# Block-sparse attention and a gated convolution FFN on one core: the two middle batches convolved whole, in a token order shared by q and k

## The chip, the cores and the metric

The kernel runs on one core of a Trainium2 chip. The time is the device time of one execution in microseconds (us). Six runs of the kernel before gave 215.57 us as median (214.54 to 216.39). One execution was profiled: 216.15 us, of which the span from the first to the last instruction is 214.4 us. The granted TensorE clock was 0.999.

## The reference

Inputs: q, k and v of shape (4, 8, 768, 64) in float32, a table of three sampled key blocks for each of 24 query blocks, and three FFN weights. Cut to what matters:

```python
scores = (q @ k.T) / sqrt(64)                       # per batch and head, 768 x 768
mask = |qblock - kblock| <= 1 or block in {0, 23} or sampled
attn = softmax(where(mask, scores, -1e9))
x = (attn @ v) heads side by side                   # (4, 768, 512)
h = relu(x @ w_in)                                  # (4, 768, 1024)
conv[s] = cw[0]*h[s-1] + cw[1]*h[s] + cw[2]*h[s+1]  # along the tokens, per channel
out = (h * sigmoid(conv)) @ w_out                   # (4, 768, 512)
```

The kernel computes all 768 x 768 scores. It adds the mask in the score matmul itself: rows 64 to 87 of the operands hold, for each token, an indicator of its block on the key side and the mask values of its block on the query side. The sigmoid is computed as a tanh of half the argument.

## The kernel before, in words

**Halves and units.** The work is cut into 8 halves (`n`): batch `b` and token half `g`. A half is 18 *units* of eight 128x128 score blocks: score matmuls into a PSUM tile `st` (L678), one exponential over 128x1024 on ACT (L685) into `pt`, and eight matmuls of the probabilities with v into `av` (L705). Units are numbered from 0 to 143 through the kernel. After 4.5 units a pair of heads is complete: DVE takes the reciprocal of the row sums (L629) and scales the result into `xtok` (L631), which SP turns by a transposing DMA into `xT` (L652); for the first half, PE turns it.

**Heads.** For each of 16 pairs of heads (`P`), POOL issues the q, k and v loads, which also cast to bf16 (L492). The q and k of the first `NPE` = 6 pairs are transposed by PE and copied by DVE (L533, L539). For later pairs SP issues two transposing DMAs into a staging tile `tmp` (L581), and DVE copies it into the slot's tiles `et` and `ot` (L424). There are `NSLOT` = 6 slots. The mask rows of slots 2 to 5 are copied from slot 0 by SP's DMAs (L445).

**Token order.** k and v put tokens 6p to 6p+5 on partition p. q puts tokens 3p to 3p+2 of each half there, so that the tokens of one half lie in three columns of 128.

**FFN of a half.** 8 blocks of 128 channels. FFN1 is four matmuls of 384 tokens (L729), then a relu on ACT or DVE (L740, L742) into `hE`. For a pair of blocks POOL adds the neighbours at the edges of the three columns (L829 to L835), and DVE forms the convolution: per tap two 384-wide multiplies (L753), two 768-wide adds (L759); ACT takes a tanh (L769); DVE adds 1 (L772) and multiplies by `hE` into `gT` (L781). The last token of half 0 needs the first of half 1, so it is saved (L844) and joined later by four small instructions (L859 to L867). FFN2 is eight matmuls for each of three token blocks (L799), a copy to `o2s` and a store by SP (L340).

**What sets the order.** All of this is put down as operations with a duration, a priority, dependencies and buffers (`Op`, `Buf`, `Pool_`). `Scheduler.forward` plays it through with one queue per engine, and one called `DQ` for the DMA engines; `backward` gives new priorities from the ends that follow; this is repeated `PASSES` = 12 times. The engines' programs are then written in the planned order, and each engine carries out its program in that order. So constants such as `OFF` (when a half's FFN is due), `XLAT` and `TLAT` (what a transposing DMA is thought to take after its issue), `load_u` (the unit at which a pair's loads may be issued) or the buffer counts change the order of instructions on all engines, and their waits.

Of the kernel before, what the change touches and what calls it, by code (L numbers as in the profile page):

```python
# [24 lines left out]
class Op:  # L25
    __slots__ = ("alts", "fn", "deps", "prio", "lat", "allocs", "earliest", "pend", "outs", "ready",
                 "start", "end", "eng", "key", "uses")

    def __init__(self, alts, fn, prio, deps, lat, earliest):
        self.alts, self.fn, self.prio = alts, fn, prio  # L30
        self.deps = deps
        self.lat = lat
        self.allocs, self.uses = [], []
        self.earliest = earliest
        self.outs = []
        self.start = self.end = self.eng = None
# [12 lines left out]
FLEX = 0.0345  # L49
LAT = {"PE": 0.23, "ACT": 0.20, "DVE": 0.16, "POOL": 0.20, "SP": 0.0, "DQ": 1.9}  # L50
OWN = {"PE": 0.0, "ACT": 0.12, "DVE": 0.11, "POOL": 0.10, "SP": 0.0, "DQ": 0.0}


class Scheduler:
# [22 lines left out]
    def forward(self):  # L77
# [11 lines left out]
        while left:  # L89
# [27 lines left out]
            for e, t in free.items():  # L117
                be = None
                for o in cand:
# [5 lines left out]
                    k = (s, o.prio, o.key)  # L125
                    if be is None or k < be[0]:
                        be = (k, o, e)
                if be is not None:
                    k2 = (be[0][0], be[0][1], be[0][2], be[0][0] + be[1].alts[e])
                    if best is None or (k2[0], k2[3]) < (best[0][0], best[0][3]):  # L130
                        best = (k2, be[1], e)
            if best is None:
                raise RuntimeError("no order: buffers too few")
            k, o, e = best
            o.eng = e
            o.start = k[0]
            o.end = k[0] + o.alts[e]
# [25 lines left out]
    def backward(self, order):  # L163
# [25 lines left out]
        while ready:  # L189
# [4 lines left out]
            for j in pred[i]:  # L194
                pend[j] -= 1
                if not pend[j]:
                    ready[j] = max(0.0, max(end[m] + lat for m, lat in succ[j]))
        for o, t in zip(order, end):
            o.prio = -t
            o.outs = []  # L200
            for b in o.allocs:
# [12 lines left out]
def kernel(  # L214
# [22 lines left out]
    NPE = 6  # L237
    NWARM = 34

# [19 lines left out]
    NTMP, NVN, NNAT, NPT, NXK, NXT, NHE, NCV, NGT, NOS = 2, 3, 3, 5, 3, 4, 3, 3, 4, 4  # L259
# [7 lines left out]
    hE_t = many(NHE, [128, NFFC, 640], BF16, "hE")  # L267
    m_t = many(NCV, [128, 2, 768], BF16, "m")
    tn_t = many(NCV, [128, 768], BF16, "tn")
    gT_t = many(NGT, [128, NFFC, 384], BF16, "gT")  # L270
# [11 lines left out]
    bblkn = sb.tile([NB, 6, 128], BF16, tag="bblkn", name="bblkn")  # L282
# [36 lines left out]
    T0, PACE0, PACE1 = 8.0, 0.91, 1  # L319
    OFF = 32.0894  # L320
    XLAT, TLAT = 3.908, 9.2201
    S_FIRST, A_FIRST, R_FIRST, N_FIRST = 5.6663, -4, 0.1178, 0.842
    F1S, F2A, F2S = 0.03, 2.344, 0.191
    WO = 22.9467
    OFFL = 28
# [12 lines left out]

    def dma_h(dst, src):
        return lambda e: (nc.sync if e == "SP" else nc.scalar).dma_start(out=dst, in_=src() if callable(src) else src)  # L340

    def src_of(t, b, h):

        if t is q:
# [7 lines left out]
    def dst_of(t, tile_, pair):  # L352
        if t is not q:
            return tile_
        return tile_.rearrange("p h (g c) -> p (h g) c", g=2) if pair else tile_.rearrange("p (g c) -> p g c", g=2)

    hw = {}
    for x, (t, h) in enumerate([(q, 0), (k, 0), (q, 1), (k, 1)]):
        i_ = op({"SP": 0.46} if x % 2 == 0 else {"ACT": 0.42}, dma_h(dst_of(t, stage0[x], False), src_of(t, 0, h)),
                [-20, -20, -18, -19][x], lat=0.4)  # L360
        hw[x] = dq([0.9, 0.4, 0.9, 0.4][x], [i_], [-20, -19, -17, -18][x])
# [17 lines left out]
    def ind(base, sign, src):  # L379
        return lambda e: nc.gpsimd.affine_select(  # L380
            out=bblkn, in_=src, compare_op=ALU.is_ge, fill=0.0, base=base,
            pattern=[[384 * sign, 2], [sign, 3], [3 * sign, 128]], channel_multiplier=-32 * sign)
# [30 lines left out]
    def w24(e):  # L413
        w = st_t[b_w.index]
        nc.tensor.matmul(out=w[0:NB, 0:384], lhsT=aadd, rhs=bblkn[:, 0:6:2, :], start=True, stop=True)
        nc.tensor.matmul(out=w[0:NB, 512:896], lhsT=aadd, rhs=bblkn[:, 1:6:2, :], start=True, stop=True)
# [9 lines left out]

    def k_rows(t, cs, b0):

        def fn(e):
            for (u, c0, n, at) in cs:  # L430
                src = bblkn.rearrange("k (g c) (j u) -> k u c g j", g=2, u=2)[:, u, c0:c0 + 2 * n - 1:2]
                dst = t[64:88, 1, 0, at:at + n].rearrange("k c (g j) -> k c g j", g=2)
# [495 lines left out]
```

The softmax here doesn't subtract the row's maximum and nothing guards it: scores larger than these inputs give would overflow.

## Time and profile before

| | |
|---|---|
| median of 6 runs | 215.57 us |
| profiled execution, its span | 216.15 us, 214.4 us |
| PE busy | 199.6 us, 93% |
| DVE busy | 189.7 us, 88%, 541 instructions |
| ACT busy | 182.3 us, 85%, 227 instructions |
| POOL busy | 81.3 us, 38% |
| first and last exponential start | 8.35 us, 183.1 us |
| the 192 multiplies of the convolution | 56.9 us |
| the 64 adds of the convolution | 35.2 us |
| DMA queues, share of 16 engines' span | POOL's 44.6%, SP's and ACT's 31.6% |

Busy times are what the profiler records of instructions. On DVE and PE the record of one instruction runs on after the next has begun, so the mean of a group is longer than what one instruction adds to a sequence. The chain shows pieces without overlap. The 40 slices of the page are 5.4 us each.

### The profile page before, as it was taken

Reading aid. Unit: us, or ns where it says so; the run is one execution under the profiler, and the core shown is the slowest. Engines: PE = TensorE matmul, PEld = TensorE weight load, DVE = VectorE, ACT = ScalarE, POOL = GpSimd, SP = SyncE. Lnnn points to the kernel's source line nnn. Section 1 sums busy time; section 2 is a strip of 40 time slices with the busy share of each in tenths; the row PEclk is TensorE's granted clock in tenths of the full one; section 3 lists DMA queues with packets and bytes.
Section 4 is the critical chain, followed back from the end, with each engine's and each line's share of the span. In section 5 each row is a group of like instructions: output and inputs, shape, how many; then the busy total and the mean of one; then the engine's idle time right before and its main releaser. Section 6 shows DMA issues by size and latency. Waiting matters only on the chain.

```text
span 214.4 us, 6605 instructions
## 1 busy us (share of the span) xinstructions
PE 199.6 (93%) x2596; PEld 150.3 (70%) x2596; DVE 189.7 (88%) x541; ACT 182.3 (85%) x227; POOL 81.3 (38%) x174
## 2 busy tenths in 40 slices
PE   7998999997999979999889999989999999998992
PEld 4787879885778857788668667667776788554441
DVE  5977539999999998398999999999999999999972
ACT  4598999999989989999988799889999999674541
POOL 8995216435524721264276302421241012443300
PEclk9999999999999999999999999999999999999999
DMA  6999998999999996999986993002100230022223
GB/s 167 146 181 198 200 202 118 125 151 166 176 111 215 144 116 83 148 182 189 166 119 114 129 195 107 18 21 66 53 23 21 75 112 21 21 95 101 99 98 147
DMA packets 50519, 25.84 MB, mean 120 GB/s; under 512 B 36320, under 2 KB 47352, under 8 KB 50488
## 3 DMA queue, kind: packets, MB, share of 16 engines
q0 software_dynamic: 18464, 11.14, 44.6%
q1 hardware_dynamic: 31592, 13.75, 31.6%
q10 hardware_dynamic: 432, 0.52, 0.8%
q8 instruction: 20, 0.33, 0.6%
q14 instruction: 11, 0.09, 0.2%
HBM read 23.08 MB, written 6.29 MB: 137 GB/s over the span
## 4 chain that ended last, share of the span: by engine, by line
DVE 60%; PE 10%; DMA 8%; POOL 6%; ACT 5%; issue 5%; SPq 3%; ACTq 0%; POOLq 0%; DVEq 0%
DVE m L753 19%; DVE m L759 11%; DVE hE L742 7%; DVE gT L781 6%; ACT pt L685 5%; DMA tmp<-nat 4%; DVE xtok L631 4%; PE st L678 4%; DVE tn L772 4%; DMA nat<-in_k_dram 4%; DVE o2s L424 2%; PE st L799 2%; POOL nat L492 2%; PE mix L799 2%; SPq L581 2%
## 5 line engine op out<-in xcount | busy, mean ns | idle before, releaser
L685 ACT ACTIVATE pt<-st 128x1024 bf16<-128x1024 f32 x144 | 141.9, 1039 | 7.5 <-PE st L678 6.2
L705 PE MATMUL av<-vt,pt 128*128 128x65 bf16 x1152 | 57.9, 193 | 0.6 <-ACT pt L685 0.2
L753 DVE TENSOR_SCALAR m<-hE,cw 128x384 bf16<-128x384 bf16 x192 | 56.9, 346 | 0.2
L705 PEld LDWEIGHTS <-pt 128*128 128x128 bf16 x1152 | 50.4, 97 | 5.0 <-ACT pt L685 0.7
L729 PE MATMUL mix<-xT,winb 128*128 128x384 bf16 x240 | 48.3, 325 | 2.8 <-DVE hE L742 1.8
L829 POOL COPY hE<-hE 128x254 bf16<-128x254 bf16 x32 | 18.2, 567 | 75.3 <-DVE hE L742 51.1
L799 PE MATMUL mix<-woutb,gT 128*128 128x512 bf16 x168 | 44.0, 379 | 1.8 <-DVE gT L781 1.4
L678 PE MATMUL st<-ot 88*128 88x128 bf16 (+1 forms) x224 | 42.5, 234 | 0.2
L678 PE MATMUL st<-et,ot 88*128 88x128 bf16 (+1 forms) x224 | 42.5, 234 | 0.0
L678 PE MATMUL st<-et 88*128 88x128 bf16 (+1 forms) x208 | 40.8, 239 | 1.7 <-ACT pt L685 1.7
L678 PEld LDWEIGHTS <-ot 88*128 88x128 bf16 x448 | 34.5, 97 | 10.2 <-issue 1.0
L678 PE MATMUL st<-ot,et 88*128 88x128 bf16 (+1 forms) x208 | 40.7, 239 | 0.5 <-ACT pt L685 0.4
L678 PEld LDWEIGHTS <-et 88*128 88x128 bf16 x416 | 32.3, 97 | 9.9 <-issue 3.2
L759 DVE TENSOR_TENSOR m<-m 128x768 bf16<-128x768 bf16 x64 | 35.2, 554 | 0.1
L769 ACT ACTIVATE tn<-m 128x768 bf16<-128x768 bf16 x32 | 27.7, 866 | 5.4 <-DVE m L759 5.3
L729 PEld LDWEIGHTS <-winb 128*128 128x128 bf16 x256 | 22.2, 97 | 13.8 <-issue 3.5
L799 PEld LDWEIGHTS <-gT 128*128 128x128 bf16 x200 | 16.5, 98 | 15.5 <-DVE gT L781 3.1
L742 DVE TENSOR_SCALAR hE<-mix 128x384 bf16<-128x384 f32 x37 | 20.2, 548 | 3.9 <-PE mix L729 3.8
L781 DVE TENSOR_TENSOR gT<-tn,hE 128x768 bf16<-128x768 bf16 x32 | 17.9, 563 | 0.1
L631 DVE TENSOR_TENSOR xtok<-av,rcp 128x384 bf16<-128x384 f32 x32 | 17.6, 550 | 0.3
L492 POOL DMA_DIRECT2D vn<-in_v_dram x16 | 11.4, 714 | 11.9 <-DVE vt L519 8.7
L740 ACT ACTIVATE hE<-mix 128x384 bf16<-128x384 f32 x23 | 11.9, 518 | 4.0 <-PE mix L729 3.3
(76 smaller groups left out, 172.0 us busy)
## 6 DMA issues: line engine op xcount, KB each, us to landing
out_dram<-o2s SPq DMA_DIRECT2D x23, 256.0 KB, 2.2
vn<-in_v_dram POOLq DMA_DIRECT2D x16, 192.0 KB, 6.9
nat<-in_q_dram POOLq DMA_DIRECT2D x15, 192.0 KB, 6.3
nat<-in_k_dram POOLq DMA_DIRECT2D x15, 192.0 KB, 6.2
winb<-in_moe_w_in_dram POOLq DMA_DIRECT2D x2, 512.0 KB, 11.0
woutb<-in_moe_w_out_dram POOLq DMA_DIRECT2D x2, 512.0 KB, 9.6
xT<-xtok SPq DMA_TRANSPOSE x27, 8.7
o2s<-in_k_dram ACTq DMA_DIRECT2D x2, 192.0 KB
```

The lines of the kernel that those rows point to most:

```text
L631: nm = op({"DVE": 0.475}, lambda e: nc.vector.tensor_tensor(out=xtok_t[xk.index].rearrange("p c h d -> p h c d"), in0=o_of()[:, :, :, 0:64 ...
L678: nc.tensor.matmul(out=st_t[stb.index][:, 128 * x:128 * (x + n_)], lhsT=QK[kc % 2][s][0:88, 1, hh, kc // 2, :], rhs=QK[par][s][0:88, 0, hh ...
L685: e_op = op({"ACT": t_act(1024)}, lambda e, stb=stb, ptb=ptb: nc.scalar.activation(out=pt_t[ptb.index], in_=st_t[stb.index], func=AF.Exp, ...
L705: nc.tensor.matmul(out=av_t[av_buf[(n, P % 4)].index][:, off:off + 65], lhsT=pt_t[ptb.index][:, 128 * x:128 * x + 128], rhs=VT[P % NSLOT][ ...
L729: nc.tensor.matmul(out=tiles[hb.index][:, 0:384], lhsT=winb[:, fc, 128 * ffc:128 * ffc + 128], rhs=xT_t[xt_buf[n].index][:, fc, :], start= ...
L742: nc.vector.tensor_scalar(out=dst, in0=src, scalar1=0.5, scalar2=0.0, op0=ALU.mult, op1=ALU.max)
L753: nc.vector.tensor_scalar(out=m_t[cb.index][:, slot, o0:o1], in0=src, scalar1=w, scalar2=None, op0=ALU.mult)
L759: nc.vector.tensor_tensor(out=m[:, 0], in0=m[:, 0], in1=m[:, 1], op=ALU.add)
L769: th = op({"ACT": 0.745}, lambda e: nc.scalar.activation(out=tn_t[cb.index], in_=m_t[cb.index][:, 0], func=AF.Tanh, bias=0.0, scale=0.5), ...
L781: nc.vector.tensor_tensor(out=o, in0=t, in1=h, op=ALU.mult)
L799: nc.tensor.matmul(out=acc()[:, 0:o1 - o0], lhsT=gT_t[gb.index][:, ffc, 128 * c:128 * c + 128], rhs=woutb[:, ffc, o0:o1], start=(ffc == 0) ...
L829: nc.gpsimd.tensor_copy(out=h[:, f0:f0 + 2, 1:128], in_=h[:, f0:f0 + 2, 384:511])
```

## The change

- **Middle batches whole.** `NARROW = (0, 3)`: batches 0 and 3 keep their two halves. In batches 1 and 2 q is loaded in the order of k (tokens 6p to 6p+5 on partition p), so that all 768 tokens form six columns. Both halves' relus go to one `hE` tile of 1024 columns, and each pair of channel blocks is convolved once: multiplies of 768, adds, tanh, "+1" and gate of 1536. The join of the two halves goes there. A batch's convolution starts when the relus of both of its halves are there. `gT` holds a batch.
- **Mask rows in two orders.** The query rows differ between the two orders. Slots 4 and 5 are made for the wide order and slots 0 to 3 for the narrow one, by DVE and POOL copies in place of the eight SP DMAs. When a slot changes order (pairs 6 to 9 and 12 to 15), SP issues two DMAs that rewrite its query rows. A small tile `rows` keeps the narrow ones.
- **Buffers.** `tmp` 2 to 3, `vn` 3 to 4, `nat` 3 to 4, `pt` 5 to 6; `hE` 3 to 2 (wider), `m` 3 to 2 (wider, `tn` is now its second half), `gT` 4 of a half to 2 of a batch.
- **Heads.** `NPE` 6 to 5: one pair more goes through the transposing DMAs.
- **Last half.** The PE transpose of its last head pair goes through a `st` tile.
- **Plan.** Each SP DMA is now an issue on SP and a transfer in the queue `DQ` (`sp_dma`), and a POOL load has a lag of 0.7 ahead of its transfer. Loads are issued up to `AHEAD` = 12 us before the backward pass needs them, in place of the units in `load_u`; w_out's loads too. Within a short time (`PATIENCE`) an engine takes the operation of highest priority, not the earliest. `FLEX` is 0, and the due times have other values.

The diff, cut to its core:

```diff
-FLEX = 0.0345
+FLEX = 0
+PATIENCE = {"PE": 0.19703813709435516, "ACT": 0.17782688815051345, "DVE": 0.16527914149207706}
...
-                    k = (s, o.prio, o.key)
+                    k = (o.ready, 0.0, o.key) if e == "DQ" else (max(s, t + PATIENCE.get(e, 0.0)), o.prio, o.key)
...
+            if o.ahead is not None:
+                o.earliest = span - t - o.ahead
...
-    NPE = 6
+    NARROW = (0, 3)
+    AHEAD = 12.0
+    NPE = 5
...
-    NTMP, NVN, NNAT, NPT, NXK, NXT, NHE, NCV, NGT, NOS = 2, 3, 3, 5, 3, 4, 3, 3, 4, 4
+    NTMP, NVN, NNAT, NPT, NXK, NXT, NHE, NCV, NGT, NOS = 3, 4, 4, 6, 3, 4, 2, 2, 2, 4
...
-    hE_t = many(NHE, [128, NFFC, 640], BF16, "hE")
-    m_t = many(NCV, [128, 2, 768], BF16, "m")
-    tn_t = many(NCV, [128, 768], BF16, "tn")
-    gT_t = many(NGT, [128, NFFC, 384], BF16, "gT")
+    hE_t = many(NHE, [128, NFFC, 1024], BF16, "hE")
+    m_t = many(NCV, [128, 2, 1536], BF16, "m")
+    gT_t = many(NGT, [128, NFFC, 768], BF16, "gT")
...
-    T0, PACE0, PACE1 = 8.0, 0.91, 1
-    OFF = 32.0894
-    XLAT, TLAT = 3.908, 9.2201
+    T0, PACE0, PACE1 = 8.0, 0.9118010899200953, 1.1331461284649915
+    OFF = 13.381043458283791
+    XLAT, TLAT = 1.6316194834047222, 0.5097704649884637
...
+    def sp_dma(fn, sp, dur, prio, deps, lat, alloc=None, uses=(), by="SP"):
+        i_ = op({by: sp}, fn, prio, deps, lat=0.1, alloc=alloc, uses=uses)
+        return op({"DQ": dur}, None, prio, [i_], lat=lat, uses=list(uses) + ([alloc] if alloc else []))
...
-        if t is q:
+        if t is q and b in NARROW:
...
-            else:
-                m[s] = op({"SP": 0.46}, rows_to(t[s], t[0]), T(4.5 * s) - 6, [m[0]], lat=6.0,
-                          earliest=T(18 + 2 * s) if s > 3 else 0.0)
+            else:
+                m[s] = op({"DVE": 0.58}, rows_by(t[s], t[0]), T(4.5 * s) - 2.5, [m[0]])
+        m[4] = op({"DVE": 0.3}, lambda e, t=t: copy_to(e, t[4][64:88, 0, 1], t[4][64:88, 0, 0]), T(14), [qn, kn])
+        m[5] = op({"DVE": 0.58}, rows_by(t[5], t[4]), T(15), [m[4]])
...
-        i_ = op({"POOL": 0.8}, lambda e: nc.gpsimd.dma_start(out=dst(), in_=src), prio,
-                list(deps) + [gate], lat=0.0, alloc=alloc, uses=uses, earliest=early)
-        return i_, op({"DQ": dur}, None, prio, [i_], lat=lat or 2.4, uses=(([alloc] if alloc else []) + list(uses)))
+        i_ = op({"POOL": 0.75}, lambda e: nc.gpsimd.dma_start(out=dst(), in_=src), prio,
+                list(deps) + [gate], lat=0.0, alloc=alloc, uses=uses, earliest=T(max(0, prio) * 8) if ahead else 0.0)
+        i_.ahead = ahead
+        lag = op({"LAG": 0.7}, None, prio, [i_], lat=0.1)
+        return i_, op({"DQ": dur}, None, prio, [lag], lat=2.6, uses=(([alloc] if alloc else []) + list(uses)))
...
+    def other_rows(P):
+        s = P % NSLOT
+        if P < NSLOT or (P // 4 in NARROW) == ((P - NSLOT) // 4 in NARROW):
+            return []
+        ops = []
+        copied = [m[x] for m in (e_mask, o_mask) for x in range(1, 4)]
+        for par, t in enumerate((ET, OT)):
+            def fn(e, par=par, t=t):
+                dst = t[s][64:88, 0].rearrange("k h c s -> k h (c s)")
+                src = t[4][64:88, 0].rearrange("k h c s -> k h (c s)")
+                if P // 4 in NARROW:
+                    src = narrow_rows[:, par].rearrange("k c s -> k (c s)").unsqueeze(1).broadcast_to([NB, 2, 384])
+                nc.sync.dma_start(out=dst, in_=src)
+            first = not ops
+            ops.append(sp_dma(fn, 0.5, 0.5, T(first_u[P]) - 8,
+                              [narrow_op[par], wide_rows[par], slot_first.get(P - 1)] + copied + ops, 1.5,
+                              alloc=slot_b[P] if first else None, uses=[] if first else [slot_b[P]]))
+        slot_first[P] = ops[0]
+        return ops
...
         def mul(x, slot):
             def fn(e):
-                for (o0, o1, src, w) in muls(x):
-                    nc.vector.tensor_scalar(out=m_t[cb.index][:, slot, o0:o1], in0=src, scalar1=w, scalar2=None,
-                                            op0=ALU.mult)
+                for y in range(2):
+                    nc.vector.tensor_scalar(
+                        out=m_of(slot)[:, w * y:w * y + w], in0=hE_t[hb.index][:, f0 + y, 128 * x:128 * x + w],
+                        scalar1=cw[:, x, f0 + y:f0 + y + 1], scalar2=None, op0=ALU.mult)
...
+        wide = b not in NARROW
+        heb, gtb = he_buf[n], gt_buf[b]
+        w = 768 if wide else 384
...
-            if ffc % 2 == 0:
+            if ffc % 2 == 0 or wide and g == 0:
                 continue
...
-        if g == 1:
+        if g == 1 and not wide:
```

## The prediction

> **What bounds the kernel now.** I read the page from the top: busy shares, slices, the chain, then sums by stretch, then waits.
>
> ```profile
> PE 199.6 (93%) x2596; PEld 150.3 (70%) x2596; DVE 189.7 (88%) x541; ACT 182.3 (85%) x227; POOL 81.3 (38%) x174
> ...
> DVE  5977539999999998398999999999999999999972
> ACT  4598999999989989999988799889999999674541
> ...
> DVE 60%; PE 10%; DMA 8%; POOL 6%; ACT 5%; issue 5%; SPq 3%; ACTq 0%; POOLq 0%; DVEq 0%
> ```
>
> Three engines are nearly full, and DVE carries 60% of the chain. Its slices are full from about 105 to 205 us and have holes before 40 us and at 80 to 100. The sums by stretch (busy us of PE, PEld, DVE, ACT, POOL) say the same:
>
> ```profile
> 0.00:101.00 101.00, 94.52 (x1381) 77.03 (x1382) 82.61 (x233) 90.28 (x106) 50.33 (x94) 1.00 1.18 158
> 101.00:184.00 83.00, 79.59 (x1079) 60.74 (x1077) 82.33 (x238) 77.93 (x99) 23.41 (x62) 1.00 0.49 84
> ...
> 173.50:212.00 38.50, 35.95 (x289) 20.94 (x287) 35.06 (x101) 24.23 (x38) 10.34 (x28) 1.00 0.22 81
> ```
>
> From 101 to 184 us DVE idles 0.7 of 83 us. In the last 38.5 us PE and DVE are both about full. So what DVE loses is worth its full price only until PE becomes the limit. The waits between 80 and 100 us show what DVE stood for: FFN matmuls and attention, not loads.
>
> ```profile
> DVE rcp L629 <- PE av L705: 2.3, 1, 2.3
> DVE hE L742 <- PE mix L729: 1.9, 2, 1.3
> ```
>
> In the whole run DVE waits 0.9 us for one transposed load (et from tmp). More buffers for loads alone can win about that.
>
> **Prices.** The rows of groups give records that overlap; the chain gives what one instruction costs in a row of them:
>
> ```profile
> 46.62 0.92 DVE m L753 x4
> 47.54 0.47 DVE m L759
> ...
> 51.87 0.27 DVE tn L772
> 52.13 0.47 DVE m L759
> 52.60 0.47 DVE gT L781
> ```
>
> So a 384-wide multiply costs 0.23, a 768-wide add or gate 0.47, the 768-wide "+1" 0.27. A wider form is not in the trace except the 64x1536 copies (0.47 in the chain at best) against the 128x768 copy to vt (0.27): 0.20 for 768 more elements in the fast mode, 0.10 for 384. A 768-wide multiply is then 0.33 and a 1536-wide "+1" 0.47. [...]
>
> **The merged convolution (batches 1 and 2), DVE.** For one pair of filter blocks and both halves: before 12 x 0.23 + 4 x 0.47 + 2 x 0.27 + 2 x 0.47 = 6.12. After 6 x 0.33 + 2 x 0.87 + 0.47 + 0.87 = 5.06. The difference, 1.06, times 8 pairs is 8.5 us. [...] The join of two halves (about 0.3 us a batch in the chain) goes in two batches: 0.6.
>
> **Other DVE work.** Heads 5 to 4 by PE transposes: 4 copies of 0.55 out, 2 of 0.55 in, -1.1. In the new order of instructions two casts and two output copies move to ACT and one relu comes: -1.5. The mask rows of slots 2 to 5, until now SP DMAs, become DVE copies: six more of 24x1536 (0.47), about three of 768 and five of 384: +4.5, bounded above by the one such copy in the trace, which ran beside a POOL copy and took 0.87 (then +7). They fall before about 30 us, where DVE idles some 10 us; the first ones stand ahead of the second pair's head copies, with 0.7 us to spare at 12 us, so 0 to 1 us can reach the exponentials. Then pair 3's k load, which lands at 19.0 us, gates anyway. DVE in all: -8.5 - 0.6 - 1.1 - 1.5 + 4.5 = -7.2; counting the new order with the averages of this trace (a multiply 0.27, the slow ones beside POOL copies included) I get -9.7.
>
> [...] POOL's edge copies (hE from hE) take between 0.39 and 1.33 us, median 0.48, so something holds them at times. [...]
>
> **ACT and PE.** A tanh costs 0.74; from 1024-wide exp (0.90) and 384-wide relu (0.37) the slope is 0.83 ns an element, so 1536 wide is 1.38 and eight of these save 0.8. Moved copies eat it: ACT 0. PE loses 12 small transposes, 0.5.
>
> **Queues.** POOL issues woutb's two loads directly after winb's. These took 2.6 us each in the stream (winb landed at 23.5 and 26.2), so the next q and k land about 5 us later than now (27.2, 28.2), at some 33. Pair 5's transposes (6.8 us to landing) are then there at 40; the new order has its copy on DVE at unit 28 to 31, 38 to 41 us: 0 to 2 us, on an engine that has slack there. SP now carries sixteen mask-row DMAs for slots that change between the two token orders. Each waits for a slot's last score matmul, and the xT transposes queue behind it; FFN1 reads xT more than 10 units later, which hides it. Without that cover it would be about 1 us each. Staging of three instead of two tmp buffers ends the waits of SP at 84 to 90 us: at most the 0.9.
>
> **Where the work falls.** This decides. I cut the two orders of instructions at unit 81 (its exp starts at 101 us; PE ends at 211.3) and sum each engine with start-to-start prices: matmul 0.03 for 65 columns, 0.055 per 128, 0.162 for 384, 0.216 for 512; DVE and ACT as above, with the average waits. Before: PE 83.4 + 103.2, DVE 85.9 + 103.2, ACT 85.0 + 88.6. After: PE 80.5 + 105.7, DVE 84.2 + 95.2, ACT 84.2 + 89.7. So the second part holds 8 us less DVE work but 2.5 us more PE work: a wide batch's convolution waits for its second half, and out matmuls slide to the end (after the last score matmul PE has 28.6 us left, before 25.9; DVE 21.2 and 21.1).
>
> **Likeliest.** Second part: before, 103.2 us of DVE work fill 101.6 us (104.1 to 205.7), which is the bound. After, PE is: its 105.7 at the fullness of the last stretch now (36.3 counted of 37.5 us, 0.97) need 109; it took 110.3, so -1.3. First part: I take the 1.7 that DVE loses, near ACT's 0.8 and short of PE's 2.9, since every engine is short of work there in turn. A further 0.5 for the SP waits. Sum -3.5 against a profiled span of 214.4 (execution 216.15). The median shown is 215.57, so **212.0**; 212.7 if only that execution counted. Own range 210 to 214.4.
>
> **Rivals.**
> *PE without holes* (0.13): the looser DVE lets PE run through: first part -2.9, second 105.7 against 110.3, -4.6: 208. DVE's full 9.7 cannot come, PE forbids it. For it: DVE ends nearly every wait of PE now. Against: PE at 0.94 over the second part is already high.
> [...]
> *Bunching makes it slower* (0.28): the convolution of batch 1 comes in one lump. Between the norms of units 90 and 94.5 the new order has 10.7 us of DVE work where PE has 4.2. The two av buffers let DVE be late by one group, about 5 us; after that PE's in-order queue stands, with scores, exps and FFN behind it. That is 5 us once, 2 at units 126 to 135 (DVE 13.4, PE 11.5) and 2 of the present holes: 105.7 + 9 = 114.7, +4.4, less 1.7: 218.3. It decides from 4.6 + 1.7 = 6.3 us of PE idle in the second part. For it: adding the largest engine load of every nine units gives 126.9 us for units 36 to 135 now (measured 127.1: 46.6 to 173.7) and 122.5 after, but 3.2 more in the last nine units and 2.5 more in the nine-unit stretches before unit 36. Against: with stretches of 18 units the same sum falls 9 us up to unit 126, and DVE can lag between norms.
>
> **Numbers.** Likeliest 0.42, no holes 0.13, cancels 0.17, bunching 0.28. A difference under 0.5% (1.1 us) cannot be told from none. Faster 0.42 + 0.13 = 0.55, same 0.17, slower 0.28. Range 207.0 to 218.5: it takes in the bunching at its price and PE without holes, leaving out what lies beyond both.
>
> **What would show it.** Right: DVE's busy sum falls by 7 to 10 us to about 181; PE's stays; the slices of DVE show holes between units 60 and 90; 768-wide multiplies near 0.40 in record, 1536-wide adds near 0.95; the last exp starts 3 to 6 us earlier than 183.1, the stretch after it is about 2 us longer, and PE's share of the chain grows well over 10%. Wrong: PE waiting for DVE norms (rcp, xtok) for several us near unit 95; et or ot from tmp waiting for DMA by more than 3 us; a first exp later than 9.5 us; more than 15 us of DVE idle after unit 81 with the exp pace unchanged.

## The result, and the profile after

The changed kernel runs as long as the one before: a median of 216.06 us (35 runs) against 215.02 us (72 runs of the kernel before beside them), ratio 0.999, 95% interval 0.997 to 1.001. The ratio leaves out disturbed executions, more than 1.5% above the fastest: 14 of the 35 of the changed kernel, whose other 21 have a median of 215.0 us. The forecast of 212.0 us, clearly faster, was wrong. The profiled execution took 215.68 us, its span is 214.0 us (before: 216.15 and 214.4).

From the page of the changed kernel: busy sums, slices of DVE and ACT, the chain.

```profile
PE 200.8 (94%) x2590; PEld 149.9 (70%) x2590; DVE 184.6 (86%) x463; ACT 184.1 (86%) x220; POOL 74.0 (35%) x150
...
DVE  7899756999978599957449999997999999999962
ACT  4798999999999869987999999999999999574560
...
DVE 52%; PE 22%; issue 9%; ACT 6%; DMA 6%; SPq 2%; POOL 1%; DVEq 0%; POOLq 0%
```

DVE lost 5 us of busy time and 78 instructions, PE's share of the chain has gone from 10% to 22%. DMA has 6% of the chain (before 8%), now almost all of it transposes into `tmp` (5.8%; before 4.5%), and DVE has slices with 4 or 5 tenths at 70 to 75 us and at 91 to 112 us. The sums by stretch of the changed kernel, cut as those of before in the prediction (busy us of PE, PEld, DVE, ACT, POOL):

```profile
0.00:101.00 101.00, 92.98 (x1333) 74.77 (x1334) 85.60 (x229) 89.70 (x103) 45.81 (x87) 1.00 1.07 160
101.00:184.00 83.00, 82.22 (x1128) 62.77 (x1127) 75.50 (x166) 79.12 (x90) 21.60 (x43) 1.00 0.47 84
...
173.50:212.00 38.50, 36.05 (x255) 19.70 (x253) 33.99 (x97) 24.22 (x40) 12.33 (x32) 1.00 0.25 91
```

From 101 to 184 us the two engines have changed places: PE is now busy 82.2 of 83 us (before 79.6) and DVE 75.5 (before 82.3). That much of the forecast came. Before 101 us PE has 1.5 us less to do, and yet unit 81 comes no earlier. The starts of the exponentials show where time was won and lost (us from the span's start):

| exponential of unit | 9 | 54 | 81 | 117 | 143 | end |
|---|---|---|---|---|---|---|
| before | 18.1 | 69.2 | 101.0 | 151.0 | 183.1 | 214.4 |
| changed | 19.1 | 65.5 | 101.8 | 145.3 | 180.8 | 214.0 |
| difference | +1.0 | -3.7 | +0.8 | -5.7 | -2.3 | -0.4 |

The profile of the kernel before is a late one of its kind. Its execution took 216.15 us, 1.1 more than the median of 72 runs, and four kernels of the experiments that differ from it only behind unit 81 have unit 9 at 17.4 to 18.8 us, unit 54 at 67.5 to 69.0 and unit 81 at 99.3 to 100.8. So the gains in the table are up to 1.7 us too large.

Against this profile two gains come and go. 3.7 us are there at unit 54 and gone at unit 81; 6.5 us more come from there to unit 117 and most is handed back before the end. The waits of the changed kernel from 60 to 101 us name the first loss (us in total, times, longest):

```profile
DVE et L443 <- DMA tmp<-nat: 4.7, 2, 2.5
PE av L757 <- DVE xtok L678: 3.4, 2, 2.8
```

The same in time: a piece of the chain, then DVE and PE (start, us, what; in brackets the idle time ahead of it).

```profile
64.01 2.84 SPq L626
...
66.95 5.52 DMA tmp<-nat
...
72.56 0.55 DVE et L443
...
78.64 0.47 DVE xtok L678
```

```profile
72.56 0.55 DVE L443 COPY et<-tmp 64x1536 bf16<-64x1536 bf16 x1 [2.22 <-DMA tmp<-nat]
```

```profile
79.16 0.28 PE L757 MATMUL av<-vt,pt 128*128 128x65 bf16 x4 [2.82 <-DVE xtok L678]
```

DVE stands for 2.2 us before the copy of pair 8 out of `tmp`, which is needed only at unit 72, about 18 us later. Everything behind it on DVE's in-order queue is late, `xtok` among it, and PE stands for `xtok` 6 us after that. At 96.7 us the copy of pair 11 does the same (2.5 us), some 10 us ahead of its scores. The changed plan takes a transposing DMA to land some 1.9 us after its issue (0.1 to its queue, 1.25 on it, 0.51 after it; the kernel before: 9.2). The answer of the trace on the tile `tmp` has what it takes (minimum, median, maximum of those whose landing the trace has):

```profile
L626 SPq DMA_TRANSPOSE tmp<-nat x22: 1210/1246/2844, 30.3 to 130.6; - x22
...
DMA to landing us min/median/max: 5.1/6.5/7.9
```

So the planner put copies into DVE's order several us before their data could be there.

### The profile page after: what moved, and what is told of

It is laid out like the page before. It is cut to its first block, busy times and chain, and to the rows that moved or that the text cites. A ratio compares the mean times of both kernels' runs of the same rounds, so it can differ in the third digit from the quotient of the medians.

```text
span 214.0 us, 6523 instructions
## 1 busy us (share of the span) xinstructions
PE 200.8 (94%) x2590; PEld 149.9 (70%) x2590; DVE 184.6 (86%) x463; ACT 184.1 (86%) x220; POOL 74.0 (35%) x150
## 4 chain that ended last, share of the span: by engine, by line
DVE 52%; PE 22%; issue 9%; ACT 6%; DMA 6%; SPq 2%; POOL 1%; DVEq 0%; POOLq 0%
DVE m L811 17%; DVE m L817 10%; PE st L730 8%; DMA tmp<-nat 6%; ACT pt L737 6%; DVE gT L830 5%; DVE hE L794 5%; DVE xtok L678 4%; PE mix L853 4%; PE mix L781 3%; PE av L757 3%; DVE m L828 3%; DVE ot L443 2%; SPq L626 2%; PE st L853 2%
## 5 line engine op out<-in xcount | busy, mean ns | idle before, releaser
L737 ACT ACTIVATE pt<-st 128x1024 bf16<-128x1024 f32 x144 | 140.0, 1035 | 6.8 <-PE st L730 5.7
L757 PE MATMUL av<-vt,pt 128*128 128x65 bf16 x1152 | 56.5, 193 | 4.1 <-DVE xtok L678 4.1
L889 POOL COPY hE<-hE 128x254 bf16<-128x254 bf16 x24 | 16.2, 674 | 104.1 <-DVE hE L794 50.9
L811 DVE TENSOR_SCALAR m<-hE,cw 128x384 bf16<-128x384 bf16 (+1 forms) x144 | 47.0, 376 | 0.5
L730 PEld LDWEIGHTS <-ot 88*128 88x128 bf16 x448 | 33.1, 97 | 6.4 <-issue 1.6
L826 ACT ACTIVATE m<-m 128x768 bf16<-128x768 bf16 (+1 forms) x24 | 25.6, 1067 | 9.7 <-DVE m L817 9.6
L817 DVE TENSOR_TENSOR m<-m 128x768 bf16<-128x768 bf16 (+1 forms) x48 | 32.8, 688 | 0.4
L853 PEld LDWEIGHTS <-gT 128*128 128x128 bf16 x200 | 17.6, 98 | 15.9 <-DVE gT L830 1.9
L794 DVE TENSOR_SCALAR hE<-mix 128x384 bf16<-128x384 f32 x39 | 21.3, 550 | 7.2 <-PE mix L781 7.1
L830 DVE TENSOR_TENSOR gT<-m,hE 128x768 bf16<-128x768 bf16 (+1 forms) x24 | 17.2, 716 | 0.2
L509 POOL DMA_DIRECT2D nat<-in_q_dram x15 | 11.7, 781 | 3.8 <-PE st L730 2.2
```

The costliest lines, as they stand in the source:

```text
L509: i_ = op({"POOL": 0.75}, lambda e: nc.gpsimd.dma_start(out=dst(), in_=src), prio, list(deps) + [gate], lat=0.0, alloc=alloc, uses=uses, e ...
L730: nc.tensor.matmul(out=st_t[stb.index][:, 128 * x:128 * (x + n_)], lhsT=QK[kc % 2][s][0:88, 1, hh, kc // 2, :], rhs=QK[par][s][0:88, 0, hh ...
L737: e_op = op({"ACT": t_act(1024)}, lambda e, stb=stb, ptb=ptb: nc.scalar.activation(out=pt_t[ptb.index], in_=st_t[stb.index], func=AF.Exp, ...
L757: nc.tensor.matmul(out=av_t[av_buf[(n, P % 4)].index][:, off:off + 65], lhsT=pt_t[ptb.index][:, 128 * x:128 * x + 128], rhs=VT[P % NSLOT][ ...
L794: nc.vector.tensor_scalar(out=dst, in0=src, scalar1=0.5, scalar2=0.0, op0=ALU.mult, op1=ALU.max)
L811: nc.vector.tensor_scalar(out=m_of(slot)[:, w * y:w * y + w], in0=hE_t[hb.index][:, f0 + y, 128 * x:128 * x + w], scalar1=cw[:, x, f0 + y: ...
```

## Experiments

Each row of the table at the end of this section is a median beside runs of the kernel before on the same chip. Where places are compared, they are places in the profiled executions.

**The suspected wait taken away.** Nothing is changed but the places of three copies in DVE's order: pair 8's `et` copy goes behind the first norm of half 3 (unit 58.5), pair 11's two copies behind the first norm of half 4 (unit 76.5). Their scores come at units 72 and 85.5.

```diff
-        for o in sc.run(PASSES):
+        order = sc.run(PASSES)
+        for what, behind in ((moved[8][0], moved[(3, 0)]), (moved[11][0], moved[(4, 0)]), (moved[11][1], moved[(4, 0)])):
+            order.remove(what)
+            order.insert(order.index(behind) + 1 + (what is moved[11][1]), what)
+        for o in order:
```

> The changed kernel, with three staging copies of DVE (et from tmp of head pair 8; et and ot of pair 11) written later in DVE's program, behind the norms that stood behind them; nothing else moves. Theory (late transposes): DVE stood 2.2 us at 72.6 and 2.5 us at 96.7 for transposing DMAs that the plan thought landed, and PE then waited 2.8 us for a norm; without that the exponential of unit 81 starts 3 to 4 us earlier than 101.8, and since PE is full from there on, the end comes 3 to 4 us earlier: 211 to 212, ratio to the kernel before 0.980 to 0.988. Rival (end load): whatever the first part gains is lost again behind the last units, as the 6.8 us lead at unit 126 was: within 1 us of the kernel before, 0.995 to 1.003.

213.28 us, ratio 0.9933 (0.9909 to 0.9957): faster than both kernels, and between the two expectations. It is 2.8 us less than the changed kernel's median of all runs, and 1.7 less than the 215.0. On DVE's timeline the two copies now stand without a wait:

```profile
84.71 0.63 DVE L443 COPY et<-tmp 64x1536 bf16<-64x1536 bf16 x1
...
101.83 0.54 DVE L443 COPY et<-tmp 64x1536 bf16<-64x1536 bf16 x1
```

This profiled execution started 2.4 us late (its exponential of unit 9 at 21.5 us; the last section shows what differs there); the one below with PE work added in batch 2 is the same program up to 179 us, and its profile started as the changed kernel's did: units 9, 54, 81, 117 and 143 at 19.1, 65.5, 98.8, 142.3 and 177.7 us. So all 3 us of this pair of profiles are won between units 54 and 81, and carried unchanged to the last exponential. The other experiments bear it out: from unit 9 to unit 81 the seven profiled kernels with the copies moved take 79.6 to 79.9 us, the changed kernel and the one that differs from it only later 82.7 and 84.9. Against the five profiles of the kernel before, unit 81 at 98.8 us is 0.5 to 2.2 us earlier.

**The landing time corrected in the plan instead.** One constant, after which the planner orders everything anew.

```diff
-    XLAT, TLAT = 1.6316194834047222, 0.5097704649884637
+    XLAT, TLAT = 1.6316194834047222, 5.0
```

> The changed kernel with one constant of the plan, the time that a transposing DMA of heads takes to land after its transfer, 5.0 in place of 0.51 (measured 5.1 to 7.9 from issue to landing). The whole plan is made anew with it. Theory (late transposes): DVE's waits for tmp fall from 4.7 us to under 1 and the time to 211 to 213, ratio 0.981 to 0.991. Rival (end load): the waits go and the time stays within 1 us of the kernel before. A new plan can also order other things worse, then up to 1.01.

218.36 us, ratio 1.0139 (1.0103 to 1.0174). The waits for `tmp` are gone from the profile, as they should be, but DVE now waits elsewhere, in 17 places for FFN1 (the list of waits of the whole run):

```profile
DVE hE L794 <- PE mix L781: 12.1, 17, 1.5
```

The time is beyond what either expectation allowed. A new constant is a new order of some 3,500 instructions, so this run tests the order it got and not the constant. It says that the wait can be avoided, and nothing on what it cost.

**Which engine limits the second part.** The same work, 12 more out matmuls of 512 columns (12 x 0.216 = 2.6 us of PE), in the first block of each of batch 2's out matmuls, first in the changed kernel and in the kernel before. A matmul of block 0 starts its sum afresh, so the doubled pair changes time and not the result.

```diff
-                    for ffc in (2 * a, 2 * a + 1):
+                    for ffc in ((0, 1, 0, 1) if a == 0 and n in (4, 5) else (2 * a, 2 * a + 1)):
```

> The changed kernel with the first two matmuls of each of batch 2's six output blocks done twice (12 more of 512 columns, 12 x 0.216 = 2.6 us of PE, the result the same), in the same order of instructions. Theory (PE took over as the limit): 2 to 2.6 us slower than the changed kernel. Rival (DVE is still the limit, as it was): under 0.8 us slower.

> The kernel before with the same 12 matmuls more in batch 2's output blocks. Theory (there DVE is the limit and PE has some 7 us of slack after unit 81): under 1.3 us slower than the kernel before, ratio up to 1.006. Rival (PE was the limit already): 2 to 2.6 us slower, ratio 1.010 to 1.012.

The kernel before: 215.76 us, ratio 1.0031 (1.0012 to 1.0050), +0.7 us by the ratio for 2.6: PE has slack where this work falls. The changed kernel: 220.31 us, 1.0182 (1.0092 to 1.0272). That is more than the added work, and its profile says why it can't be used: the waits up to 101 us, long before the first added matmul, had grown from the 4.7 us shown above.

```profile
DVE et L443 <- DMA tmp<-nat: 5.8, 2, 4.5
```

Both profiles have unit 54 at 65.5 us, and this one has unit 81 at 104.0 where the other has 101.8. So the wait for the landing differs from one execution to the next, and unit 81 by 2.2 us with it. The test was made again on the kernel with the three copies moved, with three edits: the same PE work in batch 2; 2.6 us of DVE work in batch 2's convolution; and, as its counterpart, 2.8 us of DVE work in the kernel before.

```diff
-                for y in range(2):
+                for y in ((0, 0, 1, 1) if x == 1 and gb is gt_buf[2] else (0, 1)):
```

> The changed kernel with its three late copies moved, and in it twelve more 512-column matmuls in batch 2's first out matmuls (12 x 0.216 = 2.6 us more PE work, the same values written again and then started afresh, so that the output is that of the first two channel blocks counted twice in those blocks). Theory (after the merge PE is the limit from unit 81 on): 2.0 to 2.6 us more than the same kernel without them (213.3): 215.3 to 215.9. Rival (PE still has slack as in the kernel before, where the same matmuls cost 0.7): 0.3 to 1.2 us more, 213.6 to 214.5.

(The sum starts afresh with the second block 0, as said above; nothing is counted twice, as that text has it.)

> The changed kernel with its three late copies moved, and in batch 2 every multiply of the middle tap done twice: 8 multiplies of 768 more, 8 x 0.33 = 2.6 us more DVE work. Theory (DVE is no longer the limit from unit 81 on): 0 to 1.0 us more than 213.3, so up to 214.3. Rival (DVE is still the limit): 2.0 to 2.6 us more, 215.3 to 215.9.

> The kernel before with 12 multiplies of 384 done twice in batch 2: 12 x 0.23 = 2.8 us more DVE work. Theory (DVE is the limit of the kernel before from unit 81 on): 2.2 to 2.8 us more than the kernel before, ratio 1.010 to 1.013. Rival (another engine or a chain over several sets the time): less than 1.2 us more, ratio under 1.0055.

Kernel before with DVE work: 218.76 us, 1.0170 (1.0110 to 1.0231), +3.5. With the copies moved, DVE work: 216.31, 1.0073 (1.0047 to 1.0100), +3.0 by the medians, +3.7 by the fastest runs (216.25 against 212.55). The work added was more than I had put down: from each start to the next, all 768-wide multiplies sum to 21.3 us against 17.2 without the eight, so these took about 4 and not 2.6; the twelve in the kernel before took about 4 as well (56.6 against 52.3) and not 2.8. So DVE work costs most of its length in both. PE work: 214.27, 0.9976 (0.9956 to 0.9996), +1.0 for 2.6. Both tests went to the rival: DVE seemed to limit still, and PE not. But the trace showed that the PE work had been put in the wrong place. Batch 2's out matmuls run after 179.5 us in that profile, whose last exponential starts at 177.7, and all but eight of them behind the last exponential in the one before; with the copies moved no exponential is late for them. So two more, with the PE work in batch 1's out matmuls (`n in (2, 3)`), which run between 139 and 173 us, and with DVE work taken away in the same stretch.

```diff
-        m2 = op({"DVE": tm}, mul(2, 1), due + 2.1, edge + [ad1], uses=[cb, hb])
-        ad2 = op({"DVE": t_d2(2 * w)}, add, due + 2.3, [ad1, m2], uses=[cb])
+        m2 = op({"DVE": tm}, skip if gb is gt_buf.get(2) else mul(2, 1), due + 2.1, edge + [ad1], uses=[cb, hb])
+        ad2 = op({"DVE": t_d2(2 * w)}, skip if gb is gt_buf.get(2) else add, due + 2.3, [ad1, m2], uses=[cb])
```

> The changed kernel with its three late copies moved, and twelve more 512-column matmuls (2.6 us) in batch 1's first out matmuls, which run between 139 and 165 us. Theory (after 149 us DVE is the limit again, PE only looks full): 0 to 1.3 us more than 213.3. Rival (PE is the limit from unit 81 on, as predicted): 2.0 to 2.6 us more.

> The changed kernel with its three late copies moved, in which batch 2's convolution leaves out its third tap (4 pairs x (0.66 + 0.87) = 6.1 us less DVE work at about 150 to 180 us; that batch's sum has two taps). Theory (DVE is the limit there): 3 to 6 us less than 213.3, up to where PE becomes the limit. Rival (PE is the limit there): 0 to 1 us less.

PE work at 139 to 173 us: 214.77, 0.9995 (0.9969 to 1.0022), +1.5 by the medians and +2.1 by the fastest runs (214.65 against 212.55); in the profile the last exponential starts at 182.1, and at 180.0 in the profile without the added work that started as late: 2.1 of 2.6. And 6.1 us of DVE work taken away win only 0.8: 212.45 (four runs), 0.9870 (0.9799 to 0.9941, an interval that reaches the 0.9933 without the cut), with the last exponential 0.3 us earlier than 177.7 and the fastest runs 0.2 apart. So PE does limit the second part. Why does DVE work cost as well? The stretch from 150 to 180 us (columns as before), first of the kernel with the extra PE work in batch 2, which up to 179 us is the kernel with the copies moved:

```profile
150.00:180.00 30.00, 30.00 (x402) 22.25 (x400) 29.96 (x69) 29.27 (x36) 9.70 (x17) 1.00 0.17 54
```

then with batch 2's third tap left out:

```profile
150.00:180.00 30.00, 30.00 (x402) 22.26 (x400) 24.65 (x57) 29.31 (x36) 7.23 (x20) 1.00 0.17 53
```

and with the eight multiplies more:

```profile
150.00:180.00 30.00, 27.08 (x355) 19.90 (x354) 29.75 (x67) 25.83 (x31) 5.15 (x13) 1.00 0.17 53
```

In the first both engines are full. Take 5 us from DVE and PE stays full with the same 402 matmuls: hardly anything is won. Give DVE more and PE gets holes of 3 us and 47 matmuls fewer. The two are level: either costs when it grows, and DVE hardly pays when it shrinks alone. Less PE work was not tried. The chain can't tell that: in 146 to 180 us of the kernel with the extra PE work, it is all PE, and in 148 to 182 us of the kernel with the copies moved, the same program 2.3 us later, it is DVE:

```profile
by line: PE st L732 30.0%; PE mix L783 28.1%; PE mix L855 21.6%; PE av L759 20.7%
```

```profile
by line: DVE m L813 31.7%; DVE m L819 17.2%; issue 13.7%; DVE gT L832 10.3%; DVE xtok L679 8.7%; DVE hE L796 7.2%; DVE m L830 6.6%; DVE rcp L677 2.7%; PE mix L783 2.0%; DVE o2s L443 0.6%; DVEq L679 0.1%
```

The same two edits were then made in the kernel before: PE work in batch 1's out matmuls (`n in (2, 3)` in the diff above; there between 119 and 165 us), and batch 2's third tap left out.

```diff
-        m2 = op({"DVE": tm}, mul(2, 1), due + 2.1, [edge[0], ad1], uses=[cb, heb])
-        ad2 = op({"DVE": t_d2(768)}, add, due + 2.3, [ad1, m2], uses=[cb])
+        two = gtb in (gt_buf.get(4), gt_buf.get(5))
+        m2 = op({"DVE": tm}, skip if two else mul(2, 1), due + 2.1, [edge[0], ad1], uses=[cb, heb])
+        ad2 = op({"DVE": t_d2(768)}, skip if two else add, due + 2.3, [ad1, m2], uses=[cb])
```

> The kernel before with twelve more 512-column matmuls (2.6 us) in batch 1's first out matmuls, which run between about 119 and 165 us; the same work cost 1.5 to 2.1 in the changed kernel with its copies moved. Theory (DVE is the only limit of the kernel before there, and the merge made PE one): 0 to 0.9 us more than the kernel before, ratio under 1.0042. Rival (PE and DVE are level there before as after): 1.5 to 2.6 us more, ratio 1.007 to 1.012.

> The kernel before, in which batch 2's convolution leaves out its third tap (8 pairs x (2 x 0.23 + 0.47) = 7.4 us less DVE work; that batch's sum has two taps). The same cut won 0.2 to 0.8 us in the changed kernel with its copies moved. Theory (DVE is the limit there before): 3 to 6 us less than the kernel before, ratio 0.972 to 0.986, up to where PE becomes the limit. Rival (PE and DVE are level before as after): 0 to 1.2 us less, ratio 0.9945 to 1.

PE work: 215.80 us, 1.0023 (1.0002 to 1.0043), +0.5 of 2.6, where the changed kernel paid 1.5 to 2.1: PE was not the limit. DVE work taken away: 213.71 us, 0.9921 (0.9898 to 0.9945), -1.6 of 7.4, between the two expectations: DVE was the limit, with PE close behind it. The stretch from 150 to 180 us of this last kernel has PE nearly full and DVE no longer:

```profile
150.00:180.00 30.00, 29.84 (x417) 23.36 (x418) 26.58 (x75) 29.70 (x40) 7.59 (x23) 1.00 0.17 48
```

So in the kernel before, 7.4 us of DVE work taken away win some 1.6 us before PE takes over.

**Where DVE's saved time lies.** Two stretches (columns as before), first of the kernel before, then of the changed one:

```profile
101.00:112.00 11.00, 9.58 (x126) 7.23 (x124) 10.94 (x29) 9.92 (x13) 5.35 (x14) 1.00 1.25 156
150.00:180.00 30.00, 29.61 (x412) 22.96 (x409) 29.75 (x90) 29.44 (x39) 6.41 (x20) 1.00 0.18 56
```

```profile
101.00:112.00 11.00, 11.00 (x166) 8.88 (x165) 4.95 (x11) 10.28 (x12) 0.00 (x0) 1.00 0.35 87
150.00:180.00 30.00, 30.00 (x397) 22.43 (x394) 29.93 (x67) 29.44 (x35) 8.84 (x18) 1.00 0.17 53
```

In the changed kernel DVE is busy 4.95 of the 11 us from 101 to 112 (before 10.94), and 29.93 of 30 from 150 to 180 (before 29.75). From 150 to 180 us both engines look full in both kernels, so only the added and removed work could tell them apart. Some 6 of the 8 us that the merge takes off the second part lie in one hole ahead of batch 1's convolution, which starts only when both halves' relus are there. To see that work in the hole is free, one copy of v that DVE makes there was done nine times:

```diff
-            nc.vector.tensor_copy(out=VT[s][:, :, :, 0:64],
-                                  in_=vn_t[vb.index].rearrange("p h (c d) -> p h c d", c=6))
+            for _ in range(9 if P == 12 else 1):
+                nc.vector.tensor_copy(out=VT[s][:, :, :, 0:64],
+                                      in_=vn_t[vb.index].rearrange("p h (c d) -> p h c d", c=6))
```

> The changed kernel with its three late copies moved, and the copy of v of pair 12 (DVE at 103.5 us, in the stretch in which DVE waits for PE) done nine times instead of once: 8 x 0.28 = 2.2 us more DVE work, about as much as the 2.6 that cost 3.0 in batch 2's convolution. Theory (DVE's saved time lies idle at 101 to 112 us and is lacking after 150): 0 to 0.8 us more than 213.3. Rival (DVE's total decides): 2 us or more.

213.05 us, 0.9906 (0.9871 to 0.9941): no cost. On DVE's timeline:

```profile
101.83 3.52 DVE L541 COPY vt<-vn 128x768 bf16<-128x768 bf16 x9
105.27 0.19 DVE L678 RECIPROCAL rcp<-av 128x6 f32<-128x6 f32 x1
```

The norm behind it is 2.7 us later than in the other kernels of this kind, the next one (110.7 us) no longer, and no exponential moves. About 3 us of DVE work are free at 102 us, where some 4 us cost 3.0 to 3.7 after 150.

**Work moved off DVE in the full stretch.** POOL is busy 8.8 of the 30 us from 150 to 180. It gets the middle tap's multiplies of three pairs of batch 2 and three of the last half.

```diff
+        for gb_, f0_, o_, m1_ in mids:
+            if gb_ is gt_buf[2] and f0_ > 0 or gb_ is gt_buf[3] and o_ and f0_ > 0:
+                m1_.eng = "POOL"
```

> The changed kernel with its three late copies moved, and the middle tap's multiplies of three pairs of blocks of batch 2 and three of the last half done by POOL, which idles there: 3 x 0.66 + 3 x 0.46 = 3.4 us less DVE work after 150 us, estimated 2.2 and 1.2 us of POOL for each pair (from its edge copies of 254 columns in 0.44). Theory (DVE is the limit there): 1 to 3 us less than 213.3, if POOL's result is not late. Rival (POOL is later than DVE would be, and DVE waits for it): 0 to 4 us more.

220.31 us, 1.0195 (1.0126 to 1.0264): 7.0 us more, beyond even the rival. My estimate of POOL was off by more than two. In the list of groups by form:

```profile
L815 POOL TENSOR_SCALAR m<-hE,cw 128x768 bf16<-128x768 bf16 x6 | 14.9, 2488 | 0.0
```

A multiply of 768 takes POOL 2.49 us where DVE takes 0.33. DVE's adds wait for these results three times, 2.8 us in all, and DVE itself is slower beside them: from 150 us on its eight 1536-wide adds take 1.14 us each in record, against 0.94 in the kernel without, and its 768-wide multiplies 0.59 against 0.43.

```profile
L821 DVE TENSOR_TENSOR m<-m 128x1536 bf16<-128x1536 bf16 x8 | 9.1, 1140 | 0.6 <-POOL m L815 0.6
```

By the run with less DVE work, the move could hardly have won more than 0.8 anyway.

**Plan and buffers without the merge.** All four batches narrow; slots 4 and 5 get the mask rows of slot 0; `hE`, `m` and their buffer counts as before.

```diff
-    NARROW = (0, 3)
+    NARROW = (0, 1, 2, 3)
```

> The changed kernel with every batch narrow: its plan, its loads, its buffers and mask rows copied by DVE stay, its merged convolution and the rewriting of mask rows go (hE, m and the number of their buffers as in the kernel before). DVE has 8.5 us more work than in the changed kernel. Theory (the merge is what frees the second part, plan and buffers only shift work): 216 to 220, with DVE busy near 192 and the last exponential 2 us or more later than the changed kernel's 180.8. Rival (the merge gains nothing, what came and went is plan and buffers): 213.5 to 216, last exponential near 180.8.

220.93 us, 1.0280 (1.0214 to 1.0346), slower as the theory had it and 0.9 us beyond its range, with more DVE work than in either kernel (the page's first line):

```profile
PE 204.5 (93%) x2588; PEld 152.4 (69%) x2588; DVE 195.5 (89%) x543; ACT 184.5 (84%) x229; POOL 84.8 (38%) x190
```

The planner ordered anew here too. From unit 81 to the end this kernel takes 115.3 us (105.1 to 220.4), the changed one 112.2: 3.1 us are lost where the merge would have saved DVE. The other 3.3 us it has lost by unit 81, where it waits for `tmp` as well (3.3 us), so the total is not the price of the merge.

| kernel | median us | runs | ratio (95%) |
|---|---|---|---|
| changed | 216.06 | 35 | 0.999 (0.997-1.001) |
| three copies moved | 213.28 | 20 | 0.9933 (0.9909-0.9957) |
| plan with the longer landing | 218.36 | 4 | 1.0139 (1.0103-1.0174) |
| before, +2.6 us PE, mostly after 180 us | 215.76 | 20 | 1.0031 (1.0012-1.0050) |
| changed, the same | 220.31 | 4 | 1.0182 (1.0092-1.0272) |
| copies moved, the same | 214.27 | 20 | 0.9976 (0.9956-0.9996) |
| copies moved, +2.6 us PE at 139-173 us | 214.77 | 20 | 0.9995 (0.9969-1.0022) |
| copies moved, 8 DVE multiplies more at 150-180 us | 216.31 | 19 | 1.0073 (1.0047-1.0100) |
| before, 12 DVE multiplies more in batch 2 | 218.76 | 4 | 1.0170 (1.0110-1.0231) |
| before, +2.6 us PE at 119-165 us | 215.80 | 20 | 1.0023 (1.0002-1.0043) |
| before, -7.4 us DVE in batch 2 | 213.71 | 20 | 0.9921 (0.9898-0.9945) |
| copies moved, -6.1 us DVE at 150-180 us | 212.45 | 4 | 0.9870 (0.9799-0.9941) |
| copies moved, +3 us DVE at 102 us | 213.05 | 10 | 0.9906 (0.9871-0.9941) |
| copies moved, six multiplies on POOL | 220.31 | 4 | 1.0195 (1.0126-1.0264) |
| all narrow | 220.93 | 4 | 1.0280 (1.0214-1.0346) |

## Why the prediction was wrong

**The step that failed is "Queues", and with it the first part of "Likeliest".** There the transposes of pair 5 were costed at 0 to 2 us "on an engine that has slack there", and the waits for loads as a gain of 0.5. Pair 5 was the wrong pair to look at. The order of instructions, which was there to be read, has the copies of pairs 8 and 11 on DVE 18 and 10 us ahead of their scores, and the profile before has 6.8 us to landing for such a DMA; set against each other, they give the wait. DVE stood 4.7 us for it and PE 3.4 us for DVE between 60 and 101 us, and unit 81 came 0.8 us later instead of 1.7 + 0.5 = 2.2 earlier. Without it unit 81 comes at 98.8 us and not at 101.8; the time of a run falls to 213.28 us, by 2.8 from the 216.06 and by 1.7 from the 215.0. The sign for it was among those given for a wrong prediction (a wait for `tmp` of more than 3 us). Pair 5's own copy, the one that was costed, came at 44.0 us without a wait.

**A second term was put at nothing: the start.** The forecast let 0 to 1 us of the mask copies reach the exponentials, took a k load to gate behind them, and left them out of its sum. In the chain of the changed kernel DVE holds nearly all of 7.6 to 18.5 us, and 4.6 us of it are mask copies (start, us, what):

```profile
8.99 1.03 DVE et L443 x2
...
10.37 1.49 DVE ot L443
...
15.46 0.69 DVE ot L443
```

Unit 9 starts at 19.1 us. In the five profiles of the kernel before it starts at 17.4 to 18.8, and in the two latest of these (18.1, which is the profile that the forecast worked from, and 18.8) a load of 7.6 or 6.8 us stands in the chain there; in the other three no load does after 5 us. The load in the forecast's profile:

```profile
11.37 7.60 DMA nat<-in_k_dram
```

Against the three without, 1.2 to 1.7 us are lost at the start. A run that takes the mask copies away was not made, so this is read from the chain alone.

**So the 2.2 us are in part luck.** With the three copies moved, unit 81 is 2.2 us earlier than in the profile that the forecast worked from, the very figure; but that profile is a late one. From unit 9 to unit 81 the gain is 2.0 to 2.5 us against the four other profiles, as large as forecast, and the start takes part of it back. By the medians the kernel with the copies moved wins 1.7 us (213.28 against 214.97) of the 3.5 forecast.

**"Likeliest", second part: right in its number, half right in its mechanism.** PE was to be the limit with 105.7/0.97 = 109 us; it runs from 101.8 to 210.8, which is 109.0. In the kernel before, its last matmul ends at 211.0 and not at the 211.3 that the forecast read, so PE took 110.0 and the gain is 1.0, not 1.3. The kernel before is limited by DVE in the middle (added PE work costs 0.5 of 2.6, 7.4 us of DVE work taken away win 1.6); in the changed one PE limits too (1.5 to 2.1 of 2.6, and DVE work taken away wins 0.2 to 0.8). What this step did not see is that DVE has no slack after 150 us all the same: added DVE work costs 3.0 to 3.7 of 4 us there, and the 8 us it saves lie in the hole at 101 to 112 us and at the end.

**"Where the work falls": right.** Out matmuls slide to the end: the stretch behind the last exponential's start takes 33.2 us, before 31.3, close to the 2 us named. That is 1.9 of the 5.3 us that the changed kernel hands back behind unit 117; the units up to 143 take the other 3.4, with PE and DVE both full. (The 5.7 us of lead at unit 117 are again against the late profile; one other profile of the kernel before has that unit at 148.5 us and not at 151.0.)

**"Prices": right.** The multiply of 768 takes 0.33 from start to start (median of 48), the add of 1536 0.87, the gate 0.87, the "+1" 0.47 and the tanh 1.37. The 0.87 that the sum takes for a 1536-wide add and gate no run of the kernel before shows; in the changed kernel it is the median of 16 adds and of 8 gates. The records of the groups are longer, as told:

```profile
L811 DVE TENSOR_SCALAR m<-hE,cw 128x768 bf16<-128x768 bf16 x48 | 18.6, 437 | 0.1
...
L817 DVE TENSOR_TENSOR m<-m 128x1536 bf16<-128x1536 bf16 x16 | 15.0, 943 | 0.0
```

**"Other DVE work": too low by some 2 us.** DVE's busy sum fell to 184.6, not to 181. The seven mask copies of 24x1536 took 0.60 (mean of four) and 0.94 (mean of three), 5.1 us in all; less the 0.9 of the one that was there before, that is 4.2 where six at 0.47 had been counted, 2.8.

**POOL's edge copies: the sum has no term for them, and needed none.** In the changed kernel five edge copies of POOL meet a 1536-wide add or gate of DVE for 0.28 us or more in the records, and each of them runs on until 0.25 us after the end of that instruction's record: they take 0.53, 0.83, 1.13, 1.06 and 2.34 us, where the longest before took 1.33. The last of them (batch 3's) stands beside a gate and an add in a row (start, us, engine, line):

```profile
172.16 2.34 POOL L889 COPY hE<-hE 128x254 bf16<-128x254 bf16 x1 [7.99 <-ACT hE L792]
```

```profile
172.44 0.94 DVE L830 TENSOR_TENSOR gT<-m,hE 128x1536 bf16<-128x1536 bf16 x1
173.30 0.94 DVE L817 TENSOR_TENSOR m<-m 128x1536 bf16<-128x1536 bf16 x1
```

The 16 edge copies of the wide batches take 0.58 us on average, all 64 before 0.51: 0.07 more, and 12 of the 16 meet no such add or gate. No wait of PE or DVE for POOL is in the list of waits after 60 us.

**Rivals.** The same time as before, "cancels" with its 0.17, is what came: the 3.7 us won by unit 54 were gone at unit 81, and of the 6.5 won from there to unit 117 most was handed back before the end. "Bunching" computed 10.7 us between the norms of units 90 and 94.5, and 10.8 were measured (116.2 to 127.0), but PE did not stand there: it waits once for `xtok`, 0.7 us, after 121 us. The two `av` buffers and other matmuls cover more than that rival allowed, as far as this profile tells. "PE without holes" came true from 101 to 184 us (82.2 of 83 busy), but PE needed 109.0 us for the second part and not 105.7.

## What to carry to other kernels

When a planner or a diff changes how long a transfer is thought to take, go through the order of the engine that waits for it, transfer by transfer: place of the waiting instruction against issue plus the landing time in the trace. A wait far ahead of its need holds up every instruction behind it on that engine: here 4.7 us of waiting put unit 81 back by 3.0. And where one engine is relieved, ask when: some 6 of the 8 us of DVE work saved lay in a hole of DVE, and after it DVE and PE were level, so that taking work from DVE alone hardly paid any more. Last, take more than one profile of the kernel before: the one used here was up to 1.7 us late at unit 81, as much as half of the gain that was forecast from it.

## What was not expected of the hardware

- The wait for the landing of the same 22 transposing DMAs differs between executions: DVE stood 4.7 us for them in one profile of the changed kernel and 5.8 in that of the same kernel with work added only much later. The runs of the changed kernel lie between 213.1 and 220.8 us; with the copies moved between 212.6 and 215.4. That the first spread comes from the landing is argued from this, not shown; the late starts of the last point may have a part in it.
- POOL multiplies 128x768 by a scalar per partition in 2.49 us, 7.5 times DVE's 0.33, while its copies of 254 columns take 0.39 at best.
- Executions of one program come in groups some 2.3 us apart: with PE work added in batch 1, 18 of 20 runs lie within 214.65 to 215.75 and two at 217.0 and 217.3. In the profiled one, of the upper group, the exponential of unit 9 starts at 21.5 us, 2.4 later than in the changed kernel's profile, and the distance is kept to unit 108. What differs is the rate of PE at the start. In this profile and in the equally late one of the kernel with the copies moved, score matmuls of 256 columns follow each other every 213 ns until about 17 us and every 108 ns after it; in the changed kernel's profile it is 108 from 8 us on. Groups of six score matmuls on the chain of the kernel with the copies moved (start, us, what):

```profile
16.64 0.85 PE st L732 x6
...
18.01 0.44 PE st L732 x6
```

Three more profiles (with unit 9 at 19.9 to 20.2 us) keep the slow rate until 13 to 15 us; where it ends at 11 us, unit 9 is not late (19.1). The profiles of the kernel before and of its four variants don't have it from 8 us on. The granted clock doesn't always show it: from 12 to 14 us it is 0.50 in those three and 1.00 in the two late ones, at the same 213 ns. No run here shows what sets the rate.
